# Exchanged head pairs, wider joins and two load queues in a one-core DeltaNet and MLP-mixer kernel

## The chip, the cores and the metric

The kernel runs on one core of a Trainium2 chip. The metric is the device time of one execution in microseconds (us). A core has five engines that run side by side and meet only at semaphores: TensorE (PE, with weight loads shown as PEld), VectorE (DVE), ScalarE (ACT), GpSimd (POOL) and SyncE (SP), which here only issues DMAs. Each engine takes its instructions in the order in which the program lists them.

## What is computed

The input is q, k, v of shape (4, 8, 768, 48) and beta of shape (4, 8, 768): 4 batches, 8 heads, 768 time steps, 48 features. Per batch and head the delta rule is run, and a token-and-channel mixer follows on the heads put side by side (384 columns):

```python
k_n = k / (norm(k) + 1e-6)
for t in range(S):
    y[:, :, t] = einsum('bhd,bhde->bhe', q[:, :, t], state)
    v_old = einsum('bhde,bhd->bhe', state, k_n[:, :, t])
    state = state + beta_t * einsum('bhd,bhe->bhde', k_n_t, v_t - v_old)
x = y with heads merged            # (4, 768, 384)
h = relu(x^T @ w_tok1) @ w_tok2    # 768 -> 256 -> 768
u = x + h^T
out = u + relu(u @ w_ch1) @ w_ch2  # 384 -> 1536 -> 384
```

## The kernel before, in words

The 768 steps of a batch are cut into 12 chunks of 64; two chunks make a unit of 128, so there are 24 units (6 per batch) and 48 chunk steps. Eight heads are four pairs p; the two heads of a pair lie on the two halves of the partitions (rows 0 to 63 and 64 to 127).

For each unit u a set of small jobs is run:

- `load_kq`, `load_v` (k and v jobs): DMAs on SP. From unit 12 on (`TU`) `load_rows` brings k and q in four DMAs each, in a layout that DVE's 32x32 transposes turn into the features-first tiles `kq` (L366); before that TensorE turns them. `stacked` (L401) brings the chunk-stacked `kst` and `v_st` in four DMAs of 48 KB each.
- `prep` (p jobs): norms of the keys, the scales `cs`, on GpSimd the mask `mb` (L497, one instruction per unit) and the scaled keys in `gm` (L514).
- `grams` (c and d jobs, one per chunk half cc): eight matmuls p_g (L440) of k and q against k, taken out of PSUM by one DVE multiplication with `mb` into `gm` (L443).
- The triangular inverse: `to_parts`, `invert` (i jobs, one per round of up to four units, long chains of small DVE pairs L661 and L666), `from_parts`, and `join` (j jobs). A join works on 32x32 blocks: `p_z` (L748), for the unit before it `p_x` in the same loop (L751), and for the last unit of a round a second loop of `p_x` (L767). ACT copies the results out in two instructions of 32x256 each (L754, L739).
- `recur` (r jobs, one per chunk step t): `p_k` (L790, eight matmuls with the state `s_t`), DVE subtracts to `rest` (L797), `p_y` and `p_w` alternating (L810, L814), ACT copies `w_t` (L820), `p_s` and the second part of `p_y` alternating (L828, L829), DVE makes the new state (L837), ACT copies `p_y` out in two halves (L842). Each step needs the state of the one before.
- `mixer` (m jobs, one per batch): large 128x128 matmuls p (L986), p_h (L999), p_c (L1066, batch 0), p_r (L958, the others) and p_o (L1088).

A matmul in float32 is two records in the trace. The small matmuls name a place in the 128x128 array: 64 rows by 64 columns (four places) or 32 by 32 (sixteen). In `p_k` before, head i of each pair uses rows i and columns i^cc: two of the four places. In `p_y` with `p_w`, and in `p_s` with `p_y`, all four are used. In a join `p_z` uses two of the sixteen places and `p_x` two others.

PSUM has eight banks: two for `prep`, two for the step (tag `seq`), one for the matmuls that only keep TensorE's clock up (`p_warm`), three for the mixer.

The order of all instructions is written out by hand in one string `order`: a word like `r26*2` runs the job r26 to its second next `yield`. Whatever stands earlier in the string stands earlier in each engine's queue. The framework adds the semaphores.

Of the kernel before, what the change touches and what calls it, by code (L numbers as in the profile page):

```python
# [23 lines left out]
def kernel(  # L24
# [73 lines left out]
    def ps_seq(shape, name):  # L98
        return psum.tile(shape, FP32, name=name, tag="seq", bufs=2)
# [34 lines left out]
    G = U // HB  # L134
    pads = const.tile([128, 2, NL, H * DP], FP32, name="pads")
# [82 lines left out]

    p_warm = psum.tile([128, 4, 128], FP32, name="p_warm", tag="warm", bufs=1)
# [122 lines left out]
    ranked = set()  # L342
    spread = set()
    keyed = set()

    def load_rows(u, i, src):


        b, c = divmod(u, NCH)
        before = [u - 1] if u > TU else [last_in(u), last_in(u + 1)]  # L350
        assert turned.issuperset([(i == 0, x) for x in before])
        rows = src[b, :, c * U : (c + 1) * U, :].rearrange(
            "(p par) (s g) d -> par s p (g d)", par=2, g=G
        )
        for par in range(2):
            for r, f in ((C * par, 0), (C * par + HB, HB)):
                nc.sync.dma_start(
                    out=rows_of[i][r : r + HB, :, 0 : G * D - f], in_=rows[par, :, :, f:]
                )
                if r == C + HB:  # L360
                    spread.add((i, u))
                yield
# [9 lines left out]
    def load_kq(u):  # L372
        b, c = divmod(u, NCH)
        kst = kst_of[slot(u)]
        if u >= TU:
            yield from load_rows(u, 0, k)
            assert last_in(u) in ranked
            yield from stacked(kst, k, u)
            yield from load_rows(u, 1, q)
            return  # L380
        for pad, src in ((kpad, k), (qpad, q)):
# [4 lines left out]
            )  # L386
            yield
            if src is k and u >= RU:
                yield from stacked(kst, k, u)

        heads = kpad[slot(u)].rearrange("t (p par) d -> t p par d", par=2)
        for cc in range(2 if u < RU else 0):
            for par in range(2):
                nc.scalar.copy(kst[PAR[par ^ cc], :, cc], heads[PAR[cc], :, par, 0:D])
                yield

    def stacked(dst, src, u):
        rows = heads_of(src, u)
        for par in range(2):
            for cc in range(2):  # L400
                nc.sync.dma_start(  # L401
                    out=dst[PAR[par ^ cc], :, cc], in_=rows[par, cc]
                )
# [30 lines left out]
    def grams(u, cc):  # L434
        kqt = kqts[place(u)]
        p_g = ps_prep([128, NP, 2, C], "p_g")
        for p in range(NP):
            for i in range(2):
                f = PAR[i] if u < TU else FEATS[i]
                nc.tensor.matmul(p_g[PAR[i ^ cc], p], kqt[f, p, cc, 0], kqt[f, p, cc])  # L440
            yield
        assert before_in(u) is None or 2 * before_in(u) + cc in walked
        nc.vector.tensor_tensor(  # L443
            out=blocks(gm_of(u))[:, :, cc, D:GW].rearrange(
                "s p (two n) -> s p two n", two=2
            ),
            in0=p_g,
            in1=made[u][:, :, cc, None, :].to_broadcast([128, NP, 2, C]), op=ALU.mult,
        )
        grammed.add((u, cc, False))  # L450
        yield

    def prep(u):
# [7 lines left out]

        ksq = work.tile([128, NB, D], FP32, name="ksq", bufs=1)
# [20 lines left out]
        if u < TU:  # L483
            p_t = ps_turn([128, NP, 2, C], "p_t")
            for p in range(NP):
                nc.tensor.transpose(p_t[:, p], kp[:, 2 * p : 2 * p + 2], ident)
            turned.add((True, u))
            yield
            nc.scalar.copy(kqt[:, :, :, 0], p_t)
        else:  # L490
# [6 lines left out]
        scaler.tensor_tensor(  # L497
            out=mb, in0=mask_c[:, None, None, :].to_broadcast([128, NP, 2, C]),
            in1=cs[:, :, :, None].to_broadcast([128, NP, 2, C]), op=ALU.mult,
        )  # L500
        yield
        if u < TU:
            p_t = ps_turn([128, NP, 2, C], "p_t")
            for p in range(NP):
                nc.tensor.transpose(p_t[:, p], qp[:, 2 * p : 2 * p + 2], ident)
            turned.add((False, u))
# [220 lines left out]
    def join(u):  # L727
# [5 lines left out]
        assert done.issuperset([(u, 0), (u, 2)])  # L733
# [6 lines left out]

        assert len(left_over) == (not first)
        before = None if first else left_over.pop()
        assert first or done.issuperset([(before, 1), (before, 3)])
        p_z = ps_prep([128, NB, HB], "p_z")
        p_x = ps_prep([128, NB, HB], "p_x") if before else None
        for nb in range(NB):
            for r, r2 in halves:
                nc.tensor.matmul(p_z[r2, nb], wt[r, nb, HB:C], t11[r, nb])  # L748
                if before:
                    w = gm_of(before)[:, :, TC]  # L750
                    nc.tensor.matmul(p_x[r, nb], zst[r2, nb], w[r2, nb, HB:C])  # L751
        yield
        for r, r2 in halves:
            nc.scalar.copy(zst[r2], p_z[r2])  # L754
        if before:
            into(p_x, gm_of(before)[:, :, TC])
            joined.add(before)
# [6 lines left out]
        p_x = ps_prep([128, NB, HB], "p_x")  # L764
        for nb in range(NB):
            for r, r2 in halves:
                nc.tensor.matmul(p_x[r, nb], zst[r2, nb], wt[r2, nb, HB:C])  # L767
        yield
        into(p_x, wt)
        joined.add(u)  # L770
        yield

    def recur(t):
# [10 lines left out]
        heads = [(p, i, PAR[i ^ cc], PAR[1 - i]) for p in range(NP) for i in range(2)]  # L784

        if c > 0:
            p_k = ps_seq([128, NP, D], "p_k")
            for p, i, r, _ in heads:
                f = FEATS[i]
                nc.tensor.matmul(p_k[r, p], kqt[f, p, cc, 0], s0[f, p])  # L790
                if i == 1:
# [6 lines left out]
                out=rest, in0=p_k, in1=vsts[u][:, :, cc], op=ALU.subtract  # L798
# [6 lines left out]
        p_y = ps_seq([128, NP, D], "p_y")  # L805
        p_w = ps_seq([128, NP, D], "p_w")
        for p, i, r, o in heads:
            if c > 0:
                f = FEATS[i]
                nc.tensor.matmul(  # L810
                    p_y[o, p], kqt[f, p, cc, 1], s0[f, p],
                    start=(p == 0), stop=False,
                )
            nc.tensor.matmul(p_w[r, p], gm[r, 2 * p + cc, TC], rest[r, p])  # L814
            if c == 0 and i == 1 and p < NP - 1:
                yield
# [3 lines left out]
        nc.scalar.copy(w_t, p_w)  # L820
# [3 lines left out]
        if on:  # L824
            p_s = ps_seq([128, NP, D], "p_s")
        for p, i, r, o in heads:
            if on:
                nc.tensor.matmul(p_s[PAR[i], p], gm[r, 2 * p + cc, 0:C], w_t[r, p])  # L828
            nc.tensor.matmul(  # L829
                p_y[o, p], gm[r, 2 * p + cc, GC], w_t[r, p],  # L830
                start=(c == 0 and p == 0), stop=(p == NP - 1),
# [3 lines left out]
        if on:  # L835
            if c > 0:
                nc.vector.tensor_tensor(out=s1, in0=s0, in1=p_s, op=ALU.subtract)  # L837
            else:
                nc.vector.tensor_copy(out=s1, in_=p_s)
            yield  # L840
        for i in range(2):
            nc.scalar.mul(  # L842
                y[:, :, D * i : D * i + D], p_y[PAR[1 - i]], 1.0 if c else -1.0
# [21 lines left out]
    def sum_weights():  # L865
# [5 lines left out]

        a = {(j, k): (j, k) for j in range(3) for k in range(NCB)}
# [293 lines left out]
    p3 d2 t1*3 x p3*7 c3 k4*5 k7 w13 w18*2 d3*2 v1*2 v0*2 c3*3 v0 c3 d3*3 t0 p4*2  # L1166
    t2*3 x t3*2 p4*2 x t3 i0*2 w13 p4*2 w18 w17*2 i0 k4 i0*9 p4 i0*2 p4*2 c4 k8
    c4*3 w13*2 w6*2 k5*2 v0 k6 k5*2 i0*2 d4*2 k5 x z d4*3 c4 z*2 p5*2 k5 t4 p5 h0
    h1 h0 w8*2 h1 Y i0 f0 Y p4 f1 h2*2 p5*3 f0*2 w6 h0*5 k6*5 p6 z f2*2 k8*3 p5 w6
    p5 p3 p5 j0*3 f1*2 h1*5 j0*2 w8*2 w17 f2 h2*3 v0 t4*2 w17 r0*5 p6 h2*2 c5*2 v1  # L1170
    w11*2 j1 p5 k7*2 c5 k7 c5 r0 c5 r0*2 w14*2 v1 w11*2 k7*2 p7 d5*5 r1*5 w14*2
    p6*2 t5 j1 t5*2 r1*2 j1 j2 p7 h3*2 r1*3 p6*3 i1*2 r2*5 k8*2 f3*2 w9 k9*3 j1*2
    v2*2 i1*3 j2*2 r2*2 f3 i1*2 p6*3 w16 v2 w16*3 r2*2 h3 r2 i1 d6 r3*5 i1*2 w9*3
    v2 d6 h3 v2 w0 h3*2 r3 h3 d6*2 w0 d6 j3 c6*5 r3*4 w0 j2 w0 p8*2 j2 r4 p8 r4*4
    k9*3 j3*2 r4*2 i1*2 w24 i1*2 p7*7 r4 c7 r4 r5*5 k10 p9 k10 p9 c7 r4 c7*3 i1
    w5*2 p7 r5*2 w24*3 r5*3 j3*2 i1 r6*4 w26 v3*5 p9 k11 r6 d7*5 w26*3 p8*3 t6*2
    r6*2 w5*2 p8*4 v4*2 t6 i1 r6*3 h5*2 h4*2 k10*2 f4*3 c8*2 k10 p10 w28*2 c8*2 r7
    c8 r7*3 d8*4 p9 d8 w28 h4*5 p9 t6 r7*2 j4 w28 p9*3 r7*2 p9 w7 d9 w7 v4*2 f5*2
    w27*2 w7*2 d9*4 c9*2 f5 c9*3 t7*2 t8 r7*2 t7*2 j4*2 v4 p10*2 h5 r8*3 w29 t8*3
    w29 w27*2 r8*2 w29*3 j4*2 r8 w22*4 t9*4 r8*3 p10 h5*2 k11 p9 r8 h5 r9 h5 j5  # L1180
    r9*4 w4 i2*2 p10 i2*2 v5 i2 v5 w19 m0 r9 k10 j5 p10 i2 p10 v5 i2*2 w15 w4 v5*2
    w4 r9*2 i2 m0 v7 k11 j5 i2 k11*2 r9 v7 j5 p10 i2 r10 v7 i2 w15*2 i2 k12 r10*3
    w15 r10 r9 m0 j5 r10*3 i2*3 r10 p10 d10 c10*3 w25 i2 c10 d10*2 w19 k12 w4 k11
    r11*3 k12*2 w19 k12 i2 r11 r10 m0 r11 i2 r11*2 d10 Y i2*3 r11 w12 r11 i2*2
    k12*3 Y w19 w21 v6 i2 v6 i2*2 m0 i2 k12 i2*2 k12*2 w12 v6 i2*2 Y v6*2 m0*2 v7
    p12*2 m0*2 c10 m0 p11*2 f6 w21 p11 f6*2 m0*2 w12*2 f7*2 m0 f7 w21 p10 m0 p11*2
    d10 w21 m0 p12 m0 j6*2 f6 p11 j6 f8*2 w25 m0 f7 f8 w23 f8 p11 j7*3 w25 p12 m0
    w25*2 r12*2 v7 r12*3 j8*2 w31 r12 t10 w23*2 t10 j8 f9*2 m0 w23 r12 r13 w23 w32
    f9 k12 r13*2 t10*2 r13 f9 p12 p11 w31*3 r12 w30 k13 p11*2 k13 m0 r13*2 d11 k13
    d11 c11*2 r13 w32*3 r13*2 d11 w30 r13 w20*2 c11 k13*2 c11*2 w30*2 r14*2 k13 d11  # L1190
    k13 d11 r14*3 p12*2 w29 m0*4 w20*2 v8 r14 k13 d12 r14 c12 d12 c12 d12 p13 c12
    d12*2 k13*2 r14 p13*2 r14*2 m0 k13*2 v8*2 r15 w23 c12*2 w25 r15*4 p12 p13*2 v8
    w33 t11 j9 m0*2 w31 r15 p13*2 t11 t12 k14*2 m0 k14 m0*2 w31 r15 m0 r15 p13
    r15*2 c13*2 w31 k14*2 d13 c13 t11 d13 c13 d13 r16 d13 r16 c13 k14 d13 w33*2 v8
# [84 lines left out]
```

## Time and profile before

| | us |
|---|---|
| median of 3 runs | 639.93 (639.85 to 643.66) |
| the profiled execution | 638.03 |
| its span, first to last instruction | 636.3 |
| TensorE's mean granted clock in it | 0.981 |

How to read the lines that follow. "x16" is a count of records. A group's row gives line, engine, operation, output and inputs, shapes, then busy time and mean nanoseconds, then the idle time ahead of the group with what ended it. In the view of waits a row reads: who waited for whom, microseconds in total, how often, the longest. In the view of windows each engine has its busy time and number of records in that stretch; PE's busy time counts a matmul from its start to a modelled end, so matmuls that overlap leave it at 100%. In the timeline a row is start, length, engine and what ran.

### The profile page before, as it was taken

Reading aid. Unit: us, or ns where it says so; the run is one execution under the profiler, and the core shown is the slowest. Engines: PE = TensorE matmul, PEld = TensorE weight load, DVE = VectorE, ACT = ScalarE, POOL = GpSimd, SP = SyncE. Lnnn points to the kernel's source line nnn. Section 1 sums busy time; section 2 is a strip of 40 time slices with the busy share of each in tenths; the row PEclk is TensorE's granted clock in tenths of the full one; section 3 lists DMA queues with packets and bytes.
Section 4 is the critical chain, followed back from the end, with each engine's and each line's share of the span. In section 5 each row is a group of like instructions: output and inputs, shape, how many; then the busy total and the mean of one; then the engine's idle time right before and its main releaser. Section 6 shows DMA issues by size and latency. Waiting matters only on the chain.

```text
span 636.3 us, 21488 instructions
## 1 busy us (share of the span) xinstructions
PE 606.3 (95%) x9132; PEld 529.0 (83%) x9132; DVE 447.3 (70%) x1132; ACT 259.5 (41%) x631; POOL 108.7 (17%) x146
## 2 busy tenths in 40 slices
PE   8488798899999999999999999999999999999997
PEld 5367676667898988958999999769999987999997
DVE  4987876966899568988969987785627253373643
ACT  7758886447422242125623333135244230223240
POOL 2348364235301113021110010101010000000000
PEclk9878997899999999999999999999999999999999
DMA  9787568646442444354444033202020000000000
GB/s 201 131 145 170 138 133 206 151 111 155 104 111 60 92 110 92 81 131 79 92 103 101 13 94 49 66 10 38 2 54 2 27 2 0 26 1 26 1 26 26
DMA packets 135776, 50.27 MB, mean 79 GB/s; under 512 B 114656, under 2 KB 130144, under 8 KB 135680
## 3 DMA queue, kind: packets, MB, share of 16 engines
q1 hardware_dynamic: 135680, 48.89, 34.5%
q8 instruction: 72, 1.18, 0.8%
q14 instruction: 24, 0.20, 0.1%
HBM read 39.42 MB, written 9.44 MB: 77 GB/s over the span
## 4 chain that ended last, share of the span: by engine, by line
PE 81%; DVE 7%; ACT 5%; DMA 3%; issue 2%; SPq 1%; POOL 0%; DVEq 0%; ACTq 0%; POOLq 0%
PE p_o L1088 26%; PE p_r L958 19%; PE p_c L1066 7%; PE p L986 5%; PE p_h L999 5%; PE p_k L790 3%; PE p_s L828 3%; PE p_g L440 3%; PE p_y L810 3%; DMA d<-in_moe_w_ch_dram 1%; PE p_z L748 1%; PE p_ut L1009 1%; PE p_w L814 1%; DVE sub L661 1%; PE p_y L829 1%
## 5 line engine op out<-in xcount | busy, mean ns | idle before, releaser
L1088 PE MATMUL p_o<-wc,r 128*128 128x192 f32 x720 | 125.8, 329 | 0.6 <-ACT u_t L1013 0.6
L1088 PEld LDWEIGHTS p_o<-wc,r 128*128 128x128 f32 x720 | 116.7, 190 | 2.7 <-ACT u_t L1013 1.1
L970 DVE TENSOR_TENSOR r<-r,p_r 128x512 f32<-128x512 f32 x90 | 59.7, 684 | 39.9 <-PE p_r L958 38.8
L1017 DVE TENSOR_TENSOR xb<-xb,p_o 128x192 f32<-128x192 f32 x84 | 29.3, 350 | 59.5 <-PE p_o L1088 59.3
L967 ACT COPY r<-p_r 128x512 f32<-128x512 f32 x54 | 31.5, 584 | 91.4 <-PE p_r L958 89.8
L666 DVE TENSOR_TENSOR x<-x,sub 128x84 f32<-128x84 f32 (+24 forms) x178 | 59.6, 335 | 6.1
L661 DVE TENSOR_TENSOR sub<-x 128x84 f32<-128x84 f32 (+24 forms) x178 | 58.4, 328 | 7.1 <-DMA x<-n_dram 2.8
L1066 PE MATMUL p_c<-u_t,wc 128*128 128x256 f32 x216 | 51.2, 387 | 0.2 <-ACT u_t L1013 0.2
L1088 PE MATMUL p_o<-wc,s 128*128 128x192 f32 x288 | 50.5, 329 | 0.3 <-DVE xb L1017 0.3
L414 POOL TENSOR_TENSOR v_st<-v_st,nrm 128x384 f32<-128x384 f32 x24 | 20.6, 859 | 174.6 <-DMA v_st<-in_v_dram 140.7
L1088 PEld LDWEIGHTS p_o<-wc,s 128*128 128x128 f32 x288 | 46.8, 190 | 1.2 <-DVE xb L1017 0.6
L820 ACT COPY w_t<-p_w 128x192 f32<-128x192 f32 x48 | 15.3, 319 | 73.2 <-PE p_w L814 72.5
L1066 PEld LDWEIGHTS p_c<-u_t,wc 128*128 128x128 f32 x216 | 39.6, 190 | 5.9 <-ACT u_t L1013 0.4
L974 ACT ACTIVATE r<-r 128x512 f32<-128x512 f32 x54 | 33.8, 630 | 25.6 <-DVE r L970 25.3
L440 PE MATMUL p_g<-kq 48*64 48x128 f32 (+1 forms) x704 | 38.3, 290 | 3.3 <-ACT kq L509 3.3
L497 POOL TENSOR_TENSOR mb<-mask_c,cs 128x512 f32<-128x512 f32 x20 | 21.0, 1050 | 114.1 <-DVE gm L443 45.1
L842 ACT ACTIVATE xb<-p_y 64x192 f32<-64x192 f32 x96 | 31.1, 324 | 21.3 <-PE p_y L829 10.5
L958 PE MATMUL p_r<-u_t,wc 128*128 128x128 f32 x288 | 38.5, 277 | 0.0
L958 PE MATMUL p_r<-t_d,wc 128*128 128x128 f32 x288 | 37.2, 280 | 0.0
L443 DVE TENSOR_TENSOR gm<-p_g,mb 128x512 f32<-128x512 f32 x44 | 29.4, 683 | 10.0 <-PE p_g L440 7.2
L986 PE MATMUL p<-xb,w 128*128 128x384 f32 x96 | 35.6, 513 | 0.0
L958 PEld LDWEIGHTS p_r<-u_t,wc 128*128 128x128 f32 x288 | 35.3, 192 | 0.3
(177 smaller groups left out, 1200.1 us busy)
## 6 DMA issues: line engine op xcount, KB each, us to landing
d<-in_moe_w_ch_dram SPq DMA_DIRECT2D x24, 384.0 KB, 3.9
v_st<-in_v_dram SPq DMA_DIRECT2D x96, 48.0 KB, 2.5
out_dram<-xb SPq DMA_DIRECT2D x23, 192.0 KB, 1.9
kst<-in_k_dram SPq DMA_DIRECT2D x64, 48.0 KB, 3.2
n_dram<-gm SPq DMA_DIRECT2D x72, 32.0 KB, 2.4
pads<-in_k_dram SPq DMA_DIRECT2D x24, 96.0 KB, 2.4
pads<-in_q_dram SPq DMA_DIRECT2D x24, 96.0 KB, 2.5
gm<-w_dram SPq DMA_DIRECT2D x72, 32.0 KB, 2.1
```

Source lines behind the costliest of these rows:

```text
L440: nc.tensor.matmul(p_g[PAR[i ^ cc], p], kqt[f, p, cc, 0], kqt[f, p, cc])
L661: nc.vector.tensor_tensor(out=tmp, in0=y[:, :, 0:s, s : s + 1].to_broadcast([n, k, s, w]), in1=y[:, :, s : s + 1, s + 1 : m].to_broadcast( ...
L666: nc.vector.tensor_tensor(out=y[:, :, 0:s, s + 1 : m], in0=y[:, :, 0:s, s + 1 : m], in1=tmp, op=ALU.add,)
L842: nc.scalar.mul(y[:, :, D * i : D * i + D], p_y[PAR[1 - i]], 1.0 if c else -1.0)
L958: nc.tensor.matmul(p[:, i], pieces[i // width][:, at : at + 128], f[f"u{n}"], start=first and i == 0, stop=True, skip_group_check=True,)
L967: nc.scalar.copy(o, p)
L970: nc.vector.tensor_tensor(out=o, in0=o, in1=p, op=ALU.add if sign > 0 else ALU.subtract)
L974: nc.scalar.activation(o, o, ACTF.Relu)
L986: nc.tensor.matmul(p_1[dh], piece_of(w1, c, 0)[:, dh * 128 : (dh + 1) * 128], xb[:, c], start=(c == 0), stop=(c == NCH - 1),)
L999: nc.tensor.matmul(p_h, piece_of(w2, j, c * 128)[:, c * 128 : (c + 1) * 128], r1[j], start=(j == 0), stop=(j == NDH - 1),)
L1066: nc.tensor.matmul(p_c[:, k], piece_of(wc1, cb, f * 128)[:, f * 128 : (f + 1) * 128], u_t[:, cb], start=(cb == 0), stop=(cb == NCB - 1),)
L1088: nc.tensor.matmul(p, a[:, m], wc2[:, m, j], start=(start and i == 0), stop=(i == NM - 1), skip_group_check=True,)
```

## The change

It has five parts, and the diff below is cut to them.

1. For units 12 to 23 (`SWAP = 12`) the two heads of the odd pairs are exchanged: their features lie on the other half of the partitions (`load_rows` brings each parity by DMAs of its own, eight half-sized ones per tensor where there were four), and `p_k` of the odd pairs takes the two places that the even pairs leave. Places that share columns must not write one bank at once, so the results of even and odd pairs lie in two banks (`ps_split`). The rest of a unit follows: `mb` is made by two GpSimd instructions, and the DVE and ACT instructions of the step read and write the same number of elements in another order.
2. The step's PSUM is one tile of three banks with fixed places; `p_warm` has the third of them. For t >= 24 `p_k` is in banks 0 and 1, `p_y` in banks 0 and 1 beside it, `p_w` in bank 2, `p_s` in banks 1 and 2.
3. GpSimd issues the loads of `v_st` from unit 6 on and of `kst` from unit 12 on (120 DMAs); SP issues the rest.
4. Joins from unit 6 on that have a unit before them, and the last loop of a round, use eight and four 32x32 places in two banks, where they used four and two. ACT takes the results out in four instructions of half the size where it used two.
5. The string `order` is new from its fourth line on.

```diff
+    seq = psum.tile([128, 3, 512], FP32, name="seq", bufs=1)
+    p_warm = seq[:, 2].rearrange("s (m n) -> s m n", m=4)
+
+    def ps_seq(bank):
+        n = NP * D
+        return seq[:, bank, 0:n].rearrange("s (j odd d) -> s j odd d", odd=2, d=D)
+
+    def ps_split(bank, at):
+        n = NP // 2 * D
+        return seq[:, bank : bank + 2, at * n : at * n + n].rearrange(
+            "s odd (j d) -> s j odd d", d=D
+        )
...
-        for par in range(2):
-            for r, f in ((C * par, 0), (C * par + HB, HB)):
-                nc.sync.dma_start(
-                    out=rows_of[i][r : r + HB, :, 0 : G * D - f], in_=rows[par, :, :, f:]
-                )
...
+        for odd in range(2):
+            for side in range(2):
+                for r, f in ((C * side, 0), (C * side + HB, HB)):
+                    nc.sync.dma_start(
+                        out=rows_of[i][r : r + HB, odd:NP:2, 0 : G * D - f],
+                        in_=rows[odd, side ^ odd, :, :, f:],
+                    )
...
-            yield from stacked(kst, k, u)
+            for n, _ in enumerate(stacked(kst, k, u, nc.sync if u < 12 else nc.gpsimd)):
...
-        yield from stacked(v_st, v, u)
+        yield from stacked(v_st, v, u, nc.sync if u < 6 else nc.gpsimd)
...
+            for cc, picked in enumerate((slice(0, 4, 3), slice(1, 3))):
+                scaler.tensor_tensor(
+                    out=sorted_of(mb)[:, cc],
...
+        wide = u >= 6 and not first
...
+            both = [ps_prep([128, NB // 2, HB], "p_z") for _ in range(2)]
...
+            for nb in range(NB):
+                for i, (r, r2) in enumerate(halves):
+                    lo, hi = halves[i ^ nb % 2]
+                    x = both[nb % 2]
+                    nc.tensor.matmul(x[hi, nb // 2], wt[r, nb, HB:C], t11[r, nb])
...
-        heads = [(p, i, PAR[i ^ cc], PAR[1 - i]) for p in range(NP) for i in range(2)]
+        odd = u >= SWAP
+        heads = [
+            (p, i ^ (odd and p % 2), PAR[i ^ cc], PAR[1 - i ^ (odd and p % 2)])
+            for p in range(NP) for i in range(2)
+        ]
...
-            p_k = ps_seq([128, NP, D], "p_k")
+            p_k = ps_split(0, 0) if odd else ps_seq(1)
...
-        p_y = ps_seq([128, NP, D], "p_y")
-        p_w = ps_seq([128, NP, D], "p_w")
...
+        p_y = ps_split(0, 2) if odd else ps_seq(0)
+        p_w = ps_seq(2 if odd else 1)
...
-            p_s = ps_seq([128, NP, D], "p_s")
+            p_s = ps_split(1, 3) if odd else ps_seq(1)
```

More of the change, by code (lines that the diff above doesn't have):

```diff
@@ L134 @@
     G = U // HB
+    SWAP = 12
     pads = const.tile([128, 2, NL, H * DP], FP32, name="pads")
@@ L342 @@
     ranked = set()
+    keys_in = set()
+    pads_in = set()
+    held = {"t11": None, "zst": None}
     spread = set()
@@ L751, in join @@
                     nc.tensor.matmul(p_x[r, nb], zst[r2, nb], w[r2, nb, HB:C])
+        assert held["zst"] == before
+        held.update(t11=None, zst=None)
         yield
[L753 to L757, printed above, removed]
+        assert held["zst"] is None
+        held["zst"] = u
+        if wide:
+            for r, nbs, x in crossed(1):
+                nc.scalar.copy(zst[r, nbs], x)
+            if before:
+                for r, nbs, x in crossed(0):
+                    nc.scalar.copy(gm_of(before)[r, nbs, TC][:, :, HB:C], x)
+                joined.add(before)
+        else:
+            for r, r2 in halves:
+                nc.scalar.copy(zst[r2], p_z[r2])
+            if before:
+                into(p_x, gm_of(before)[:, :, TC])
+                joined.add(before)
         if not last:
@@ L797, in recur @@
             nc.vector.tensor_tensor(
-                out=rest, in0=p_k, in1=vsts[u][:, :, cc], op=ALU.subtract
+                out=split(rest), in0=p_k, in1=split(vsts[u][:, :, cc]),
+                op=ALU.subtract,
             )
@@ L819, in recur @@
         yield
-        nc.scalar.copy(w_t, p_w)
+        nc.scalar.copy(split(w_t), p_w)
         yield
@@ L870, in block_of @@
             return w_block(j, k)
+        for u in range(NL, WIDE):
+            assert slot(u) < NL or u in ranked and turned.issuperset([(True, u), (False, u)])
         a = {(j, k): (j, k) for j in range(3) for k in range(NCB)}
```

316 lines of the change are left out of this document (197 added, 119 removed).

## The prediction, made before the result was known

> **What bounds the kernel now.** I read the page first (busy shares, chain), then the busy time of each engine in four stretches, then what TensorE waits for after the start.
>
> ```profile
> PE 606.3 (95%) x9132; PEld 529.0 (83%) x9132; DVE 447.3 (70%) x1132; ACT 259.5 (41%) x631; POOL 108.7 (17%) x146
> PE 81%; DVE 7%; ACT 5%; DMA 3%; issue 2%; SPq 1%; POOL 0%; DVEq 0%; ACTq 0%; POOLq 0%
> ```
>
> The chain that ends last runs through PE for 81% of the span. By stretch (length, then busy time and records of PE, PEld, DVE, ACT, POOL, then PE's clock, DMA share, GB/s):
>
> ```profile
> 0.00:136.00 136.00, 111.27 (x2305) 85.29 (x2306) 107.12 (x281) 92.44 (x244) 55.56 (x76) 0.91 0.73 155
> 136.00:280.00 144.00, 143.08 (x2297) 122.04 (x2296) 114.72 (x288) 52.02 (x134) 31.29 (x37) 1.00 0.45 103
> 280.00:520.00 240.00, 239.60 (x3778) 216.66 (x3777) 170.75 (x438) 89.49 (x209) 21.83 (x33) 1.00 0.24 53
> 520.00:636.30 116.30, 112.40 (x757) 105.03 (x755) 54.68 (x128) 25.59 (x45) 0.00 (x0) 1.00 0.04 14
> ```
>
> Here are two kernels in one. Until 136 us PE is idle for 24.7 us (136.00 less 111.27): recurrence, inverse and weight loads wait for each other. From 136 to 520 us PE is idle for 1.3 us in 384. What PE waits for after 130 us is:
>
> ```profile
> PE p_x L751 <- issue: 0.6, 1, 0.6
> PE p_o L1088 <- ACT u_t L1013: 0.6, 2, 0.3
> PE p_w L814 <- DVE rest L797: 0.4, 1, 0.4
> PE p_o L1088 <- DVE xb L1017: 0.3, 1, 0.3
> PE p_c L1066 <- ACT u_t L1013: 0.2, 1, 0.2
> ```
>
> 2.1 us together. So from 136 us on, a microsecond less on TensorE is a microsecond off the end, until a wait of another engine opens; ahead of 136 us work taken off PE is worth nothing. Unit 6's join, after which the wide ones start, is at 139.78 us, and step t=24 at 260.38 (rows below), so all that the change takes off PE is in the bound part.
>
> **p_k (part 1 of the change).** A p_k by itself, and a p_y with p_w:
>
> ```profile
> 339.59 0.67 PE L790 MATMUL p_k<-s_t,kq 48*64 48x48 f32 x16
> 340.19 0.38 PE L958 MATMUL p_r<-t_c,lent 128*128 128x128 f32 x1
> ...
> 217.18 0.25 PE L810 MATMUL p_y<-s_t,kq 48*64 48x48 f32 x1
> ...
> 217.33 0.22 PE L810 MATMUL p_y<-s_t,kq 48*64 48x48 f32 x1
> 217.33 0.22 PE L814 MATMUL p_w<-rest,gm 64*64 64x48 f32 x1
> 217.34 0.22 PE L810 MATMUL p_y<-s_t,kq 48*64 48x48 f32 x1
> 217.35 0.22 PE L814 MATMUL p_w<-rest,gm 64*64 64x48 f32 x1
> 217.38 0.22 PE L810 MATMUL p_y<-s_t,kq 48*64 48x48 f32 x1
> ...
> 217.79 0.69 PE L748 MATMUL p_z<-t,gm 32*32 32x32 f32 x32
> ```
>
> The 16 records of p_k take 0.60 us until the next matmul starts; the 32 of p_y and p_w take 0.61 (217.18 to 217.79). On four places the records come in groups of four, one group each 0.05 to 0.06 us (217.33 to 217.38; 0.47 for eight groups), on two places in groups of two at the same step. With four places p_k needs four groups instead of eight: 4 x 0.058 = 0.23 us less. Steps with a state to read and t >= 24 are 22 (25 to 35, 37 to 47): 22 x 0.23 = 5.1 us. The last step's p_y without a p_s also spreads over four places, another 0.23. Six of the 22 share their stretch with p_g, whose matmuls fill the free places already; I take 5.0, with 3.7 (the 16 that stand alone) as lower bound and 5.3 as upper one. The other step matmuls used four places before; nothing is saved there.
>
> **Joins (part 4).**
>
> ```profile
> 220.79 0.21 PE L748 MATMUL p_z<-t,gm 32*32 32x32 f32 x1
> ...
> 221.35 0.19 PE L751 MATMUL p_x<-gm,zst 32*32 32x32 f32 x1
> 221.48 0.59 PE L1088 MATMUL p_o<-wc,r 128*128 128x192 f32 x2
> ...
> 260.38 0.67 PE L814 MATMUL p_w<-v_st,gm 64*64 64x48 f32 x16
> 260.97 0.69 PE L767 MATMUL p_x<-gm,zst 32*32 32x32 f32 x32
> 261.60 0.25 PE L828 MATMUL p_s<-w_t,gm 64*64 64x48 f32 x1
> ```
>
> 64 records on four places run from 220.79 to 221.35, 8.8 ns each, where a loop of 32 on two takes 0.63 - 0.12 (the switch, 221.35 to 221.48) = 0.51 us. So at four places the rate of issue begins to bind, and eight places can't halve the loop: neighbours start 6 to 8 ns apart (217.33, 217.33, 217.34, 217.35), which gives 64 x 6.7 = 0.43 at best and 0.56 (no gain) at worst. I take 0.49: 13 joins x 0.07 = 0.9 us, bounds 0 and 1.7. The five last loops (units 9, 13, 17, 21, 23) go from two places to four, so to the measured 8.8 ns: 32 x 8.8 = 0.28 instead of 0.51, 5 x 0.22 = 1.1 us. The Trainium skill, "TensorE: Matmul & The Clock Gate", section "Wait — 56ns, not 53.3ns?", speaks against this part: start to start never falls below about 25 ns however small the matmul. By it 64 records could not take less than 1.6 us, wider joins would give nothing, and the sum below would be 2.0 us smaller. The trace has 8.8 ns across places, so the rule holds at most for one place, and the row decides.
>
> **The order (part 5).** In the built programs the stretches of small matmuls between large ones, from the first p_c on, go from 86 to 84, and switches between 64 and 32 places from 28 to 29. A stretch costs the switch in, the switch out (0.12 above) and a slow first large matmul, by my estimate from these rows about 0.3 us: 2 x 0.3 less 0.1 is 0.5 us gained. In the first 136 us the counts ahead of the first p_h are nearly equal (DVE 265 and 266 instructions, SP 139 and 137), but their sequence is new, and that stretch is made of waits such as
>
> ```profile
> 89.87 5.33 DMA d<-in_moe_w_ch_dram
> 96.11 3.89 DMA d<-in_moe_w_ch_dram
> ...
> 127.64 8.00 PE p_h L999 x24
> ...
> 139.78 0.24 PE p_z L748 x7
> ```
>
> One such wait more or less is 4 to 5 us either way; I take zero and keep both ends.
>
> **What other engines pay.**
>
> ```profile
> L754 ACT COPY zst<-p_z 32x256 f32<-32x256 f32 x48 | 17.4, 364 | 24.7 <-PE p_x L751 16.3 <-PE p_z L748 7.7
> L717 ACT COPY gm<-p_x 16x128 f32<-16x128 f32 x16 | 4.1, 254 | 1.1 <-PE p_x L712 0.9
> L842 ACT ACTIVATE xb<-p_y 64x192 f32<-64x192 f32 x96 | 31.1, 324 | 21.3 <-PE p_y L829 10.5 <-DMA out_dram<-xb 9.2
> L837 DVE TENSOR_TENSOR s_t<-s_t,p_s 128x192 f32<-128x192 f32 x40 | 13.9, 347 | 11.1 <-PE p_y L829 10.6 <-PE p_s L828 0.4
> L497 POOL TENSOR_TENSOR mb<-mask_c,cs 128x512 f32<-128x512 f32 x20 | 21.0, 1050 | 114.1 <-DVE gm L443 45.1 <-DVE cs L476 44.2 <-DVE x L671 24.7
> ```
>
> ACT's join copies go from 62 of 0.364 to 124 of about 0.254 (the 128-element row): 31.5 instead of 22.6, 8.9 us more on an engine busy 89.49 of 240 in the main stretch; hidden, but each join holds ACT 0.3 us longer twice. Mask `mb` in two halves: GpSimd between 0.53 and 1.05 us a half, 0 to 12.6 us more over 12 units, hidden by 21.83 busy in 240. DVE's p_g multiplications keep their element count in another stride: zero, and 24 of them at 0.1 us more would still fit into its idle 69 us.
>
> What is late next is p_k's PSUM. In the built program p_k for t >= 24 waits for ACT's two copies of p_y of the step before (they share banks 0 and 1) as well as for DVE's new state. DVE needs 0.35 us, ACT 2 x 0.32 = 0.65. With 0.22 for the last matmul to end (217.33 row) and 0.1 to wake, 0.97 us must lie between the last p_s/p_y start and p_k; before it was 0.67. Most places have four p_r or more between, which are enough. Two have only a join (0.15 + 0.45 + 0.12 = 0.72) and two only p_g: about 0.25 us each, 1.0. Behind p_k everything on PE waits. The five shorter last loops stand (four of them) between p_w and p_s, where w_t's copy of 192 elements needs 0.22 + 0.32 + 0.1 = 0.64 and the loop with switches now covers 0.55: 0.1 each, 0.5. Together 1.5 us lost, bounds 0 and 0.3 x 22 = 6.6.
>
> **The moved loads (part 3).**
>
> ```profile
> v_st<-in_v_dram SPq DMA_DIRECT2D x96, 48.0 KB, 2.5
> ...
> 88.50 0.61 SPq L401
> ...
> SPq L1020 <- DVE xb L1017: 202.1, 15, 44.2
> 100.00:440.00 340.00, 335.87 (x5404) 285.44 (x5405) 275.06 (x713) 127.43 (x319) 59.42 (x78) 0.98 0.40 92
> ```
>
> SP issues 120 loads less and 96 more (eight halves for four per tensor), about as much as before; stores that wait on SP for `xb`, up to 44.2 us, no longer hold loads back. GpSimd issues 120 in roughly 100 to 440 us. No row has a DMA issued by GpSimd. The nearest is SP's, 0.61 us an issue; the far end is that GpSimd is held until landing, 2.5 us. At 0.61 it is 73 us beside 59.42 busy of 340: hidden, and I take that. A load that is queued there behind `mb` or the scaled keys waits with them, but a value tile is asked for about two steps after its buffer came free. The Trainium skill, "DMA: Bandwidth & Descriptors", section "SWDGE vs HWDGE vs iDMA", says that GpSimd writes the descriptors in software and is slower to set up; that is no row here and would matter through the second rival.
>
> **Sum.** 5.0 + 0.9 + 1.1 + 0.5 - 1.5 = 6.0 us, all behind 136 us. The profiled execution took 638.03 us (span 636.3 and 1.7 around it), so 632.0; on the median shown, 639.93, it is 633.9. I predict 633.0 us, between the two.
>
> **Rivals.**
> - *The evacuation takes it back (637 us).* Mechanism: p_k's new wait for ACT is open in most steps, since ACT is busy with 0.6 us copies of the mixer a third of the time (89.49 of 240), and late ones push p_y's copies. At the bound of 0.3 us in 22 steps 6.6 us go, and with them the whole gain of p_k. Against: the filler of most steps is over 1.1 us. The Trainium skill, "TensorEngine Tiling (Array Packing)", section "PSUM Bottleneck", warns of just that: tiling speeds up TensorE, not the reading of PSUM.
> - *GpSimd becomes the bound (650 us, slower).* Spare time on it from 100 to 440 us is 340 - 59.4 = 281 us, 2.3 us for each of 120 loads. Above that price values and keys come late, `rest` and `gm` wait on DVE, and PE with them. At 2.5 us an issue it is 300 + 59 = 359, 19 us over; less the 6.0 won, and if the mixer fills none of it, 640 + 13, some 650. Below 2.3 nothing shows. For it: the descriptors' price is in no row. Against: SP pays 0.61.
> - *The new start.* Same work in another sequence in the 136 us that wait: one weight-load wait less gives 628, one more 638.
>
> **How the numbers follow.** My forecast (gain of 4 to 9 us, 630 to 636) has 0.53; evacuation 0.14; GpSimd 0.13; the start better 0.09, worse 0.11. About 1%, 6.4 us, is what a measurement of this kernel can tell from no change: 633.5 and 646.3. My forecast is split by the first bound, so: faster 0.28 + 0.09 + a little of the rest = 0.40; slower 0.14 (GpSimd and a worse start together); within 0.46. The range of 8 in 10 goes from the better start to the worse one with some of the stalls, 626 to 645; the forecast's own is 630 to 636.
>
> **What would show it.** Right: p_k rows with 16 records about 0.37 us long until the next matmul, joins of 64 records in 0.43 to 0.56 us, loops of 32 in 0.28, PE still over 99% busy from 136 to 520 us, stage borders shifting earlier by 6 us between 140 and 520 and not before or behind. Wrong: waits of PE on ACT `xb` or `w_t` of more than 3 us in total; GpSimd issues above 2.3 us; the first p_h not at 127.64 us but 4 us off; 16-record p_k that still take 0.60.

## The result, and the profile after

The changed kernel takes 675.11 us (median of 4 runs, 671.29 to 679.02), the kernel before in the same rounds 641.77: 1.0506 times as long, 95% interval 1.0458 to 1.0554. I had predicted 633.0 us, with 626 to 645 as the range. The profiled execution took 671.29 us (span 669.5); before it was 638.03 (636.3), so 33.2 us of span are to be explained. Two runs below (the kernel before with one PSUM tile, and the new order alone) hold one execution far above their others, 1195 and 795 us, and it is the profiled one, so their traces are not read; without it their medians are 666.32 and 702.62.

The same views as before, of the changed kernel. From the page, busy shares and the chain that ends last:

```profile
PE 620.5 (93%) x9174; PEld 532.1 (79%) x9174; DVE 449.9 (67%) x1132; ACT 268.0 (40%) x693; POOL 182.9 (27%) x278
PE 67%; DVE 12%; ACT 6%; issue 3%; DMA 2%; POOL 1%; DVEq 0%; SPq 0%; ACTq 0%; POOLq 0%
```

PE's share of the chain fell from 81% to 67%; DVE and ACT took it. By stretch (length, busy time and records of PE, PEld, DVE, ACT, POOL, then PE's clock, DMA share, GB/s):

```profile
0.00:136.00 136.00, 111.82 (x2266) 83.68 (x2268) 93.86 (x250) 88.11 (x234) 58.17 (x81) 0.90 0.66 144
136.00:280.00 144.00, 139.68 (x2179) 117.49 (x2172) 114.08 (x273) 57.37 (x162) 65.68 (x100) 1.00 0.46 104
280.00:520.00 240.00, 226.21 (x3654) 197.62 (x3652) 174.31 (x455) 86.32 (x229) 59.04 (x98) 0.98 0.26 56
520.00:669.50 149.50, 142.81 (x1094) 133.34 (x1093) 67.64 (x157) 36.16 (x68) 0.00 (x0) 1.00 0.04 14
```

From 136 to 520 us PE was idle for 1.3 us; now it is idle for 4.3 + 13.8 = 18.1. The first 136 us hold less work than before (DVE 93.86 for 107.12): the start fell behind. What PE waits for after 130 us, in total, times, longest:

```profile
PE seq L905 <- ACT xb L971: 16.0, 16, 6.1
PE p_r L1091 <- ACT r L1100: 2.5, 2, 2.3
PE seq L926 <- DVE rest L912: 0.7, 1, 0.7
```

These 16.0 us are p_k (L905) waiting for ACT's copies of p_y (L971); nothing of the kind stood in the list before, and over 3 us of it was the sign that I had named for being wrong. So was the first p_h: 140.96 us, not 127.6. The first p_c of the mixer starts at 150.34 us instead of 136.92: 13.4 us are lost ahead of it, 19.8 behind it. Of the latter, adding up the times from one matmul's start to the next on PE, product by product, 14.5 lie ahead of p_k (the waits, net of what was there before) and 4.4 inside p_r; p_k itself and the joins (with their last loops) give 1.9 and 1.4 back.

What p_k and its neighbours became (engine timeline):

```profile
322.32 0.45 PE L905 MATMUL seq<-s_t,kq 48*64 48x48 f32 x16
322.70 0.49 PE L1091 MATMUL p_r<-t_d,wc 128*128 128x128 f32 x2
...
280.46 0.45 PE L862 MATMUL p_x<-gm,zst 32*32 32x32 f32 x32
280.95 0.25 PE L945 MATMUL seq<-w_t,gm 64*64 64x48 f32 x1
```

The 16 records of a p_k take 0.38 us until the next product instead of 0.60. The last loop of a round takes 0.26 us instead of 0.50, but p_s behind it (280.95) then waits for `w_t`: 0.49 from the loop's start to p_s, where it was 0.63. One step's end, with the wait:

```profile
341.58 0.22 PE L945 MATMUL seq<-w_t,gm 64*64 64x48 f32 x1
341.62 0.85 PE L465 MATMUL p_g<-kq 48*64 48x128 f32 x16
341.82 0.35 DVE L1150 TENSOR_TENSOR xb<-xb,p_o 128x192 f32<-128x192 f32 x1
342.08 0.35 DVE L959 TENSOR_TENSOR s_t<-s_t,seq 128x192 f32<-128x192 f32 x1
342.35 0.68 DVE L485 TENSOR_TENSOR gm<-p_g,mb 128x512 f32<-128x512 f32 x1
342.47 0.66 ACT L971 ACTIVATE xb<-seq 64x192 f32<-64x192 f32 x2 [1.40 <-DVE s_t L959]
343.03 0.51 ACT L507 ACTIVATE ksq<-kst 128x384 f32<-128x384 f32 x1
343.18 0.45 PE L905 MATMUL seq<-s_t,kq 48*64 48x48 f32 x16 [0.71 <-ACT xb L971]
```

This is the place to learn from. The last p_s and p_y start at 341.58. ACT is free from 341.07 on, and p_y is ready by 341.8, yet its copies start at 342.47, when DVE has read p_s (342.08 to 342.43); p_k starts when the copies are over. Two reads that have nothing to do with each other stand one behind the other, and the new state, ready at 342.43, waits 0.75 us for the output copies. In the built program 43 of ACT's 48 pairs of copies wait for DVE; before it was 2 (an expectation below says 3, a miscount).

### The profile page after: what moved, and what is told of

It is laid out like the page before. It is cut to its first block, busy times and chain, and to the rows that moved or that the text cites. A ratio compares the mean times of both kernels' runs of the same rounds, so it can differ in the third digit from the quotient of the medians.

```text
span 669.5 us, 21828 instructions
## 1 busy us (share of the span) xinstructions
PE 620.5 (93%) x9174; PEld 532.1 (79%) x9174; DVE 449.9 (67%) x1132; ACT 268.0 (40%) x693; POOL 182.9 (27%) x278
## 4 chain that ended last, share of the span: by engine, by line
PE 67%; DVE 12%; ACT 6%; issue 3%; DMA 2%; POOL 1%; DVEq 0%; SPq 0%; ACTq 0%; POOLq 0%
PE p_o L1221 19%; PE p_r L1091 16%; PE p_c L1199 6%; PE p L1119 5%; PE p_h L1132 5%; PE seq L926 3%; PE seq L905 3%; ACT xb L971 2%; PE seq L945 2%; DVE sub L717 2%; DVE x L722 2%; PE p_g L465 2%; PE seq L950 1%; DVE r L1173 1%; DVE xb L1150 1%
## 5 line engine op out<-in xcount | busy, mean ns | idle before, releaser
L424 POOL DMA_DIRECT2D v_st<-in_v_dram x72 | 44.6, 624 | 99.4 <-DVE rest L912 75.5
L971 ACT ACTIVATE xb<-seq 64x192 f32<-64x192 f32 x96 | 31.1, 324 | 88.5 <-DVE s_t L959 47.0
L1091 PE MATMUL p_r<-t_d,wc 128*128 128x128 f32 x288 | 39.5, 286 | 2.6 <-ACT r L1100 2.5
L905 PE MATMUL seq<-s_t,kq 48*64 48x48 f32 x656 | 23.9, 229 | 19.2 <-ACT xb L971 17.9
L905 PEld LDWEIGHTS seq<-s_t,kq 48*64 48x64 f32 x656 | 18.5, 137 | 27.4 <-ACT xb L971 23.1
L1091 PEld LDWEIGHTS p_r<-t_d,wc 128*128 128x128 f32 x288 | 35.2, 195 | 4.0 <-ACT r L1100 3.1
L465 PEld LDWEIGHTS p_g<-kq 48*64 48x64 f32 (+1 forms) x704 | 29.0, 140 | 11.0 <-ACT kq L565 6.8
L293 POOL TENSOR_TENSOR wc<-w_f,d 128x384 uint32<-128x384 uint32 x24 | 24.6, 1028 | 47.3 <-DVE w_f L289 14.5
```

The costliest lines, as they stand in the source:

```text
L424: queue.dma_start(out=dst[PAR[par ^ cc], :, cc], in_=rows[par, cc])
L465: nc.tensor.matmul(p_g[PAR[i ^ cc], p], kqt[f, p, half, 0], kqt[f, p, half])
L905: nc.tensor.matmul(p_k[r, p // 2, p % 2], kqt[f, p, cc, 0], s0[f, p])
L971: nc.scalar.mul(y[:, :, picked], p_y[PAR[1 - e]], 1.0 if c else -1.0,)
L1091: nc.tensor.matmul(p[:, i], pieces[i // width][:, at : at + 128], f[f"u{n}"], start=first and i == 0, stop=True, skip_group_check=True,)
```

## Theories

T1: the changed kernel puts the products of a step and the warm-up into one PSUM tile of three banks. The program then orders every reader of that tile behind the one ahead, whatever bank it reads, in all 48 steps and not only from t = 24 on. T2: the new order makes the loss. T3: GpSimd's loads come late. T4: the exchange itself costs. The experiments change them one or two at a time; times are medians beside the kernel before on the same chip.

## Experiments

**Before with one PSUM tile.**

```diff
-    def ps_seq(shape, name):
-        return psum.tile(shape, FP32, name=name, tag="seq", bufs=2)
+    seq = psum.tile([128, 3, 512], FP32, name="seq", bufs=1)
+    p_warm = seq[:, 2].rearrange("s (m n) -> s m n", m=4)
+    def ps_seq(bank):
+        return seq[:, bank, 0 : NP * D].rearrange("s (p d) -> s p d", d=D)
```

> The kernel before, with one edit: its four step products and the warm-up tile lie in one PSUM tile of three banks, as in the changed kernel up to unit 11 (p_y in bank 0, p_k, p_w and p_s in bank 1, the warm-up in bank 2). Order, loads, joins and places of the heads stay as before. In the built program 41 of ACT's 48 copies of p_y then wait for VectorE (3 before, 43 in the changed kernel). Theory T1 (the one tile ties the readers of PSUM to each other and the warm-up to the steps, and that is most of the 33 us): 652 to 668 us, the first p_h 6 us or more later than 127.6, and p_k waiting for ACT's copies of p_y by 4 us or more after 136 us. Rival T2 (the new order makes the loss, the tile costs nothing): 638 to 645 us, first p_h within 2 us of 127.6.

Measured: 666.85 us, ratio 1.0385 (1.0341 to 1.0429). The tile alone costs 25 us, which T2 does not allow. The other two signs, a late p_h and p_k's waits, are read in the run with two banks below.

**The changed kernel with own tiles and no exchange.**

```diff
-    SWAP = 12
+    SWAP = 99
-            p_k = ps_split(0, 0) if odd else ps_seq(1)
+            p_k = split3(ps_seq([128, NP, D], "p_k"))
```

> The changed kernel with the exchange undone and the PSUM tiles of the kernel before (a tile for each step product, the warm-up in its own); wide joins, loads issued by GpSimd, the split row loads and the new order stay. 2 of ACT's 48 copies of p_y wait for VectorE in the built program. T1 (one tile): the loss goes, 632 to 645 us. T2 (order): it stays, 655 to 670 us, with the first p_h near 141 us. Third theory T3 (GpSimd's issues come late): 655 to 670 as well, but with waits of VectorE on the value and key loads.

Measured: 642.26 us, ratio 1.0035 (1.0008 to 1.0063). Joins, loads and order together cost 1 to 2 us (by medians and by the ratio), so in this order neither T2 nor T3 makes the loss. In its trace (span 640.0) the first p_c starts at 140.46 us, 3.5 later than before, and from there on nothing is lost; PE is idle for 1.5 us in 380:

```profile
140.00:520.00 380.00, 378.51 (x6012) 335.35 (x6011) 287.16 (x720) 147.66 (x399) 121.62 (x182) 1.00 0.32 73
```

ACT's copies of p_y still wait here for a store of `xb` (10.0 us in all, group row below; 11.2 in the changed kernel), but after 130 us only one p_k waits for them, for 0.2 us:

```profile
L966 ACT ACTIVATE xb<-p_y 64x192 f32<-64x192 f32 x96 | 31.1, 324 | 37.5 <-PE p_y L945 22.8 <-DMA out_dram<-xb 10.0 <-PE p_s L940 1.8
```

**The new order alone**, on the kernel before (its list put in, with p_k's and the row loads' places fitted to it).

```diff
-                if i == 1:
+                if i == 1 and (p % 2 or u < 12):
                     if p == NP - 1:
                         keyed.add(t)
                     yield
...
-    p3 d2 t1*3 x p3*7 c3 k4*5 k7 w13 w18*2 d3*2 v1*2 v0*2 c3*3 v0 c3 d3*3 t0 p4*2
+    p3 d2 t1*3 x p3*6 t0 k4 x w6 k5*2 k4*2 z p3 d3*2 c3 k4*3 p4*2 k5*3 t2*3 d3*3
...
```

> The kernel before, its work issued in the changed kernel's order and nothing else (p_k and the row loads give way at the changed kernel's places, so that its list fits; four row loads as before, at every second place). T1: 636 to 646 us, since the tiles are those of before. T2: 655 to 670 us, first p_h near 141 us.

Measured: 702.78 us, ratio 1.0945 (1.0899 to 1.099). Both theories missed. But this is no case for T2, since the same order with GpSimd's loads gave 642.3: order and loads belong together. Why it is slow with SP's loads was not tried further and stays open.

**Joins and loads in the old order**: the reverse.

```diff
-                if r == PAR[1 ^ cc] and (p % 2 or u < 12):
+                if r == PAR[1 ^ cc]:
...
-    p3 d2 t1*3 x p3*6 t0 k4 x w6 k5*2 k4*2 z p3 d3*2 c3 k4*3 p4*2 k5*3 t2*3 d3*3
+    p3 d2 t1*3 x p3*7 c3 k4*5 k7 w13 w18*2 d3*2 v1*2 v0*2 c3*3 v0 c3 d3*3 t0 p4*2
...
```

> Wide joins, loads issued by GpSimd and split row loads in the order of before, with the PSUM tiles and the head places of before. T1 and T2 both: 637 to 642 us, since a join of 64 records takes 0.56 us in both traces and only the five last loops are shorter, 0.26 for 0.50 us, of which a later w_t takes about 0.15 back. T3 (GpSimd's issues are too slow): over 646 us.

Measured: 650.97 us, ratio 1.0156 (1.0123 to 1.019): above what all but T3 allowed. Its trace has the place:

```profile
156.56 1.02 POOL L285 TENSOR_TENSOR wc<-w_f,d 128x384 uint32<-128x384 uint32 x1
157.51 1.22 POOL L417 DMA_DIRECT2D kst<-in_k_dram  x2
158.74 1.34 POOL L536 TENSOR_TENSOR mb<-mask_c,cs 128x512 f32<-128x512 f32 x1
161.38 1.01 POOL L285 TENSOR_TENSOR wc<-w_f,d 128x384 uint32<-128x384 uint32 x1 [1.29 <-DVE w_f L281]
162.33 0.64 POOL L417 DMA_DIRECT2D v_st<-in_v_dram  x1
162.96 0.62 POOL L417 DMA_DIRECT2D kst<-in_k_dram  x1
...
166.87 0.52 ACT L500 ACTIVATE ksq<-kst 128x384 f32<-128x384 f32 x1 [5.44 <-DMA kst<-in_k_dram]
167.42 0.55 DVE L503 TENSOR_REDUCE ksum<-ksq 128x8 f32<-128x384 f32 x1 [5.26 <-ACT ksq L500]
167.89 0.34 DVE L955 TENSOR_TENSOR s_t<-s_t,p_s 128x192 f32<-128x192 f32 x1
168.29 0.34 PE L901 MATMUL p_k<-s_t,kq 48*64 48x48 f32 x2 [4.64 <-DVE s_t L955]
```

The issues are cheap (0.62 us), but the fourth one of this unit's key rows stands on GpSimd behind a mask and a piece of the weights, and the weights wait 1.29 us for DVE. ACT stands at the square of the keys (5.44 us), DVE's sum behind ACT, the state `s_t` behind the sum on DVE, p_k behind the state. That the loads did this and not the joins, the run of the joins alone shows below; the loads of k and q, split into halves here too, were not tried by themselves.

**The changed kernel without the exchange, one tile kept.** 

```diff
-    SWAP = 12
+    SWAP = 99
...
-                        in_=rows[odd, side ^ odd, :, :, f:],
+                        in_=rows[odd, side, :, :, f:],
```

> The changed kernel with the exchange undone (heads, loads of the rows and masks placed as before) but with its one PSUM tile of three banks kept: p_y in bank 0, p_k, p_w and p_s in bank 1, the warm-up in bank 2, for all units. It differs from the run with own tiles in the tile alone. T1 (the one tile is the loss): 660 to 675 us, first p_h near 141 us, p_k waiting for ACT's copies of p_y. Rival T4 (the exchange itself costs, by its strided operands or its shared banks): 640 to 650 us.

Measured: 682.80 us, ratio 1.0619 (1.0545 to 1.0693): 7 to 8 us more than with the exchange (by ratios and by medians), 37 to 41 more than with own tiles. That is above T1's range too, so in this order the tile costs more than I expected. T4 would need the exchange to cost; inside the one tile it gains, though the two intervals touch.

**Before, the steps in one tile of two banks, the warm-up in its own.**

```diff
+    seq = psum.tile([128, 2, 512], FP32, name="seq", bufs=1)
...
-            p_k = ps_seq([128, NP, D], "p_k")
+            p_k = ps_seq(1)
-        p_y = ps_seq([128, NP, D], "p_y")
+        p_y = ps_seq(0)
```

> The kernel before with its four step products in one PSUM tile of two banks (p_y in bank 0, the others in bank 1) and the warm-up in a tile of its own, as before. Against the run with one tile of three banks it tells what the warm-up in the same tile costs. T1 in its main form (the readers of the step products wait for each other): 652 to 666 us. T1 by way of the warm-up (steps wait for warm-up matmuls): 641 to 648 us.

Measured: 666.46 us, ratio 1.04 (1.0349 to 1.0451), as with the warm-up inside. The first p_h starts at 136.67 us, 9 us late, and what PE waits for after 130 us is what it was in the changed kernel:

```profile
PE seq L791 <- ACT xb L843: 15.0, 17, 4.2
```

**The changed kernel with the warm-up in the mixer's tiles.**

```diff
-    p_warm = seq[:, 2].rearrange("s (m n) -> s m n", m=4)
...
         while True:
+            p_warm = ps_mlp([128, 4, 128], "p_warm")
```

> The changed kernel with one edit: the warm-up matmuls write into the mixer's PSUM tiles instead of bank 2 of the steps' tile. T1 by way of the warm-up: the first p_h comes 5 us or more before 141 us and the time is 662 to 670 us. T1 in its main form, and every theory in which the warm-up plays no part: 670 to 679 us.

Measured: 668.68 us, ratio 1.0428 (1.0377 to 1.0479), and the first p_h at 136.34 us instead of 140.96. In the new order, which puts more warm-up between the steps (126 records of it, before 84), the warm-up is 5 to 6 us of the loss; the two intervals overlap, so this size is rough. In the old order it was nothing.

**Before with two fixed tiles**: the same banks as in the two-bank run, one tile for each.

```diff
-    seq = psum.tile([128, 2, 512], FP32, name="seq", bufs=1)
+    keys = psum.tile([128, NP, D], FP32, name="p_keys", bufs=1)
+    outs = psum.tile([128, NP, D], FP32, name="p_outs", bufs=1)
```

> The kernel before with the banks of its step products fixed as in the two-bank run (p_y in one bank, p_k, p_w and p_s in the other), but each bank a tile of its own. It differs from the two-bank run, 666 us, in the tile's extent alone: the banks, the matmuls and the order are the same. T1 (the ties come from the one tile): 638 to 644 us. Rival T5 (the fixed banks cost, for without turns p_k has only one place): 655 to 668 us.

Measured: 641.94 us, ratio 1.0021 (0.9997 to 1.0046). Same banks, same matmuls, same order, 24.5 us less. ACT's group of p_y copies in the two-bank run and in this one (busy, mean ns, then idle ahead of them and what ended it):

```profile
L843 ACT ACTIVATE xb<-seq 64x192 f32<-64x192 f32 x96 | 31.1, 324 | 62.0 <-DVE s_t L838 19.0 <-DVE rest L798 15.7 <-PE seq L791 15.5
```
```profile
L842 ACT ACTIVATE xb<-p_outs 64x192 f32<-64x192 f32 x96 | 31.2, 325 | 24.5 <-PE p_outs L829 11.7 <-DMA out_dram<-xb 7.9 <-DVE x L666 3.2
```

The copies cost the same; what they wait for changed from DVE's reads to the matmul that makes their data. The Trainium skill, "PSUM — Partial Sum Buffer", section "PSUM bank collisions raise a hardware error", says that two engines must not be on one bank of a partition at once. That would be a reason to order readers of one bank; here p_y and p_s lie in different banks in both runs, so the 24.5 us are no price of the banks.

**Joins alone**, in the order, loads and tiles of before.

```diff
+        wide = u >= 6 and not first
...
+                    nc.tensor.matmul(x[hi, nb // 2], wt[r, nb, HB:C], t11[r, nb])
```

> The kernel before with the wide joins and last loops alone: its order, its loads on SP, its tiles. 639 to 642 us, no difference that can be measured: joins of 64 records take 0.563 us before and after, and five last loops save 0.24 us each less the 0.15 that w_t then takes. If wide joins cost ACT's 62 further copies in the bound part (rival): 643 us or more. If the run with joins and GpSimd loads in the old order (651 us) lost its 10 us by the loads, they do not show here.

Measured: 640.58 us, ratio 1.0005 (0.9983 to 1.0027). No difference, as expected.

**The exchange in two tiles.** p_k, p_w and p_s in one tile of two banks, p_y in one bank; to make p_y fit, its odd pairs' second products are issued with the next p_k.

```diff
+    keys = psum.tile([128, 2, 512], FP32, name="p_keys", bufs=1)
+    outs = psum.tile([128, 512], FP32, name="p_outs", bufs=1)
...
+                if pending and p >= NP // 2:
+                    next(pending[0][0])
```

> The changed kernel, exchange, joins, loads and order kept, but with the products of a step in two PSUM tiles: p_k, p_w and p_s in one of two banks, p_y in one of one bank; the warm-up takes the mixer's tiles. So that p_y fits into one bank, from unit 12 on the second products of its odd pairs are issued together with the next step's p_k, and ACT's copies of p_y follow them. 2 of ACT's 48 pairs of copies wait for VectorE in the built program, and no p_k waits for ACT. T1: 634 to 644 us; p_k's gain of 4 to 5 us shows against the run with own tiles (642.3), unless p_y and p_w now wait for the later copies. T4 (the exchange itself costs): 655 to 670 us.

Measured: 652.56 us, ratio 1.0186 (1.0127 to 1.0244), between the ranges of the two theories. In this run the last step of one batch computed part of its output from the following step's `w_t`; the amount of work is the same. Mended, and one wait moved:

```diff
+        if not on and odd:
+            copy_out(0)
+            for h in od:
+                to_out(*h)
...
-    t20*2 c21 d21*2 c21*2 d21*3 c21*2 t21*4 i5 r32*2
+    t20*2 c21 d21*2 c21*2 d21*2 r32*2 d21 c21*2 t21*4 i5
```

> The run with the exchange in two tiles, mended in two places: the odd pairs' second products of a batch's last step are issued at the place of its first ones (in that run they came after the next batch's first step had written its w_t over the one that they read, so one step's output was computed from other data), and two groups of p_k's matmuls stand before unit 21's last mask multiplication instead of behind it, so that PE no longer waits there for ACT (2.4 us, behind which the granted clock fell). T1: 638 to 647 us, at most 5 to 10 us over p_k's full gain, because p_y now waits for copies that come later. If the rest of the 12 us were the exchange itself (T4): 650 us or more again.

Measured: 653.24 us, ratio 1.02 (1.0169 to 1.0231). My expectation missed, and the time lies where I had put T4: of the 33 us 22 are back and 11 stay, against the run with own tiles. No p_k waits for ACT any more, but:

```profile
441.31 0.32 PE L964 MATMUL p_outs<-w_t,gm 64*64 64x48 f32 x4
441.69 0.66 ACT L980 ACTIVATE xb<-p_outs 64x192 f32<-64x192 f32 x2 [1.77 <-PE p_outs L964]
442.37 1.06 ACT L848 COPY zst<-p_z 32x128 f32<-32x128 f32 x4
443.45 1.07 ACT L851 COPY gm<-p_z 32x128 f32<-32x128 f32 x4
444.02 0.25 PE L870 MATMUL p_x<-gm,zst 32*32 32x32 f32 x4 [2.39 <-ACT gm L851]
```

The later copies push the join's eight copies, and the last loop needs both PSUM banks of the wide join. And behind the wait the clock falls (stretches of 4 us):

```profile
440.00:444.00 4.00, 1.63 (x32) 1.38 (x32) 3.52 (x14) 2.20 (x9) 0.00 (x0) 1.00 0.00 0
444.00:448.00 4.00, 3.68 (x72) 3.42 (x73) 0.62 (x4) 0.82 (x3) 0.00 (x0) 0.52 0.32 70
448.00:452.00 4.00, 4.00 (x43) 3.83 (x41) 0.00 (x0) 2.09 (x6) 0.00 (x0) 0.63 0.32 51
```

By my estimate from these rows the clock took, on top of the 2.4 us of waiting, about 3.68 x 0.48 + 4.00 x 0.37 = 3.2 us.

**The same with the joins of before.**

```diff
-        wide = u >= 6 and not first
+        wide = False
```

> The second run of the exchange in two tiles (653 us) with all joins and last loops in the form of before. There TensorE waits 2.4 us at 441.6 us for ACT: the later copies of p_y, then the join's eight copies, and the last loop after them needs both of the join's PSUM banks; behind that wait the granted clock is 0.52 and 0.63 for 8 us. With the join of before ACT has four copies of 0.36 us there and the last loop needs one bank. Theory (the miss of 653 us comes from this place, wait and clock): the wait shrinks to 1.0 to 1.6 us, the clock stays at 1.0, and the time is 645 to 650 us. Rival (the later copies of p_y cost in every step, and the place matters little): 651 us or more.

Measured: 648.64 us, ratio 1.0109 (1.0073 to 1.0144). The wait is 1.5 us, as expected, but the clock does not stay at 1.0: it falls for a shorter time, and the next stretch is back at 1.00:

```profile
444.00:448.00 4.00, 4.00 (x54) 3.87 (x50) 0.71 (x5) 0.92 (x3) 0.00 (x0) 0.61 0.33 70
448.00:452.00 4.00, 4.00 (x72) 3.65 (x72) 1.31 (x3) 2.42 (x6) 0.00 (x0) 1.00 0.28 43
```

It is 4.6 us less by the medians; in the two traces the work from 394 to 453 us takes 2.5 us less. So the place was a part of the miss and not all of it. For the rest, the traces of the run above and of the one with own tiles: p_k's matmuls save 5.1 us, but the split second products take 4.9 us more than p_s and p_y took together, and the way into p_k 2.5 more. What the exchange gives in p_k, this layout takes back in p_y; no run tells the exchange and its layout apart without the one tile. No version beat the kernel before.

## Why the prediction was wrong

The step that failed is the one on what is late next, "p_k for t >= 24 waits for ACT's two copies of p_y of the step before". I had found the wait and priced it at 1.5 us, at most 6.6. Two things in it were wrong.

- I let ACT's copies run beside DVE's read ("DVE needs 0.35 us, ACT 2 x 0.32 = 0.65"). They run behind it: 43 pairs wait for DVE. So the chain of a step grew by all of ACT's part and by whatever ACT was doing, and the wait measured 16.0 us, the longest 6.1, where ACT's copies stood behind a store that had not landed:

```profile
291.09 0.66 ACT L971 ACTIVATE xb<-seq 64x192 f32<-64x192 f32 x2 [10.20 <-DMA out_dram<-xb]
291.81 0.68 PE L905 MATMUL seq<-s_t,kq 48*64 48x48 f32 x16 [6.08 <-ACT xb L971]
```

- I confined it to t >= 24. The tile is the same for all units, so the ties are there from the first step on (ahead of 130 us p_k waits for ACT's copies three times, 2.2 us in all, and the warm-up twice for DVE's `rest`, 2.7 us), and the first 136 us, which I had left at zero with 4 to 5 us either way, lost 13.4. Of these 3.5 are there with own tiles (order and loads; inside my bound), the other 9.9 come with the tile.

By the runs, along one path: joins, loads and order 1 to 2 us more, the one tile 37 to 41 more, the exchange in it 7 to 8 less. The spans of the four traces give 3.7 (636.3 to 640.0), 42.1 (682.1) and 12.6 (669.5), but one trace of each stands for runs that spread over up to 12 us. Each size holds for this order of steps; in the old order the tile was 25 us.

The other terms:

- p_k on four places: 0.38 us a block, as predicted (0.37). The 5 us show in the exchange in two tiles (5.1); in the changed kernel itself only 1.9 are left, beside the waits.
- Joins: I took 0.49 us for 64 records and gave 0.56 as the case of no gain. The thirteen take 0.56, as before; the rate of issue, 8.8 ns, bound. The 0.9 us were zero.
- Last loops: 0.26 (I said 0.28). Up to the next product four of the five take 0.05 to 0.14 us less than before, because `w_t` came into view (I had 0.22 less 0.1). The fifth, at 460.11 us, takes 1.68 instead of 0.62: PE waits there twice for ACT's copies of the join and once for DVE's `rest`. So this term was no gain.
- GpSimd's issue, the disputed price: I took SP's 0.61 us.

```profile
L424 POOL DMA_DIRECT2D v_st<-in_v_dram x72 | 44.6, 624 | 99.4 <-DVE rest L912 75.5 <-DVE sub L717 21.0 <-issue 2.0
```

It is 0.62 in this row (44.6 us for 72), so the rival in which GpSimd becomes the bound is refuted by its own condition (2.3 us). What a load costs there is its place in the queue: 4.64 us on PE for one of them in the old order, and behind that wait the granted clock is 0.50 from 168 to 172 us.

- The rival nearest to the truth was "the evacuation takes it back", at 637 us. Its mechanism happened and its size was bounded by the wrong model: 0.3 us in 22 steps, instead of a serial chain in each of the 44 steps that read a state. The warning that I had cited with it (the Trainium skill, "TensorEngine Tiling (Array Packing)", section "PSUM Bottleneck") is of another mechanism: the copies out of PSUM take 0.32 us as before, and only what they wait for changed.

One cost I had in no term: the clock. In the 6.1 us wait and behind it (the changed kernel, 4 us each):

```profile
285.00:289.00 4.00, 0.72 (x5) 0.43 (x3) 2.82 (x10) 0.00 (x0) 1.19 (x2) 0.90 0.15 57
289.00:293.00 4.00, 1.19 (x17) 1.01 (x18) 0.45 (x1) 1.56 (x6) 2.46 (x4) 0.50 0.37 93
293.00:297.00 4.00, 4.00 (x10) 2.15 (x9) 3.76 (x10) 0.00 (x0) 0.00 (x0) 0.75 0.28 58
```

Here, by my estimate, 1.19 x 0.50 + 4.00 x 0.25 = 1.6 us of work was lost on top of the wait.

## What to carry to other kernels

When a change merges PSUM buffers into one tile, look in the built program for what every reader of that tile waits for, before pricing anything else: reads by two engines, of banks that do not touch, were put one behind the other, and that was 25 us in one order of steps and 37 to 41 in another. Price a wait by the chain that it joins (here matmul, DVE, ACT, matmul) and by what else stands in front on the in-order engine, not by the durations of its own two copies. A load moved to another queue must be placed again in that queue's order; its issue price says little.

## What was unexpected of the hardware

- Eight 32x32 places issue no faster than four: 64 records took 0.563 us on both.
- The granted clock fell behind some short waits of PE and not behind others. Behind one of 1.5 us it shows 0.61 over the next 4 us, behind one of 2.4 us 0.52 and 0.63 over 8 (rows above). In the changed kernel one of 2.3 us, from 400.0 us on, left it at 1.00:

```profile
400.00:404.00 4.00, 1.68 (x16) 1.68 (x16) 2.22 (x9) 2.08 (x5) 0.00 (x0) 1.00 0.33 131
404.00:408.00 4.00, 4.00 (x49) 3.83 (x48) 3.11 (x8) 1.57 (x5) 2.11 (x4) 1.00 0.29 45
```

What decides between them, no run here shows. The Trainium skill, "TensorE: Matmul & The Clock Gate", section "What's actually happening", puts the fall to half rate after an idle window of about 3.4 us; the traces agree on the half (0.50 in the row from 289 us), and shorter waits were followed by it here too.
